# A convolution with a routed feed-forward layer: 512-row blocks with seven products, and sequences worked whole

## The chip, the cores and the metric

The kernel runs on one core of one Trainium2 chip. The metric is the device time of one execution in microseconds (us). Before the change three runs gave 1325.76, 1326.06 and 1327.54 us; the median is 1326.06 us.

## The reference

The input is `x` of 8 sequences x 3584 tokens x 192 channels, float32. First a lightweight convolution: each of 8 heads has 24 channels and seven taps, and a token's new value is the softmax-weighted sum of itself and the six tokens before it:

```
out = np.einsum('hk,bskhg->bshg', w, x_unf)      # 7 taps for each of 8 heads
```

Then each convolved token goes through one of eight feed-forward experts. Its expert is the argmax of eight logits, but where a "local" gate is at least 0.5 the token takes the expert of the token before it, so the choice runs along the sequence:

```
if s == 0 or local_gate[b, s] < 0.5: e = fresh_e
else:                                e = prev_e
h = np.maximum(x[b, s] @ w1[e], 0.0)             # 192 -> 1024
out[b, s] = p[e] * (h @ w2[e])                   # 1024 -> 192
```

There are 28672 tokens. Counted by expert, the reference's routing gives 3274, 3841, 3138, 3745, 3518, 3081, 4253 and 3822 tokens.

## The kernel before, in words

**Two jobs.** The side work convolves the tokens, finds their experts and scatters their rows into `slots`, a buffer in HBM that is sorted by expert. The main loop takes blocks of rows of one expert out of `slots` and puts them through the expert's two matrices. A unit is 128 rows. Rounded up by expert, the counts above are 229 units.

**Blocks.** The list `blocks` is fixed when the kernel is built; which expert and which rows a block takes is read at run time from small tables that the side work fills (`table`). Before the change there are 35 single blocks (128 rows), 87 pairs (256 rows) and 20 singles at the end: 55 + 174 = 229 units. Two spare singles stand behind a run-time branch.

**One block on TensorE.** `hidden` (line 952) multiplies the rows by the first matrix, 192 deep as three 64-row pieces, two array halves at a time (line 963), ReLU on ScalarE (line 968) writes `hT`. Then TensorE transposes the rows `xg` of the *next* block (`turn`, line 928; transposes recorded at line 359), which ScalarE copies to `xT` (line 949). Then `output` (line 973) multiplies `hT` by the second matrix (line 980); ScalarE and VectorE scale the two halves and add them into `o_sb` (lines 988, 992), and GpSimd scatters the rows to the output (line 996). TensorE takes its instructions in order: the transposes for block i+1 stand between the two products of block i.

**Transfers.** SyncE's queue loads weights (line 904, 1.5 MB a block, three blocks ahead), input (line 119) and rows (`load_rows`, line 911). The first load of a group of tokens waits until every scatter ("put", line 775) of the group into `slots` has landed. Scatters and output scatters go through GpSimd's one in-order queue.

**Side work.** 16 groups of 1792 tokens, two to a sequence. Groups 0 and 1 go through TensorE at the start. Groups 2 to 15 are convolved on VectorE: per head one ScalarE tap (line 377) and six VectorE instructions (line 387), 48 a group, 128 x 336 elements each. Then `route` transposes and multiplies by the gate (line 580, 24 matmul pairs, "logits"), finds experts and positions, and adds 14 puts to `to_put`. All of it is dealt out in the main loop by hand: `step(t)` emits about t us of side work into VectorE's queue at fixed places of a block. `ensure(i)` emits the row loads up to three blocks ahead; where the group of a block isn't routed and put yet, it goes away and tries again a block later, until only two blocks are left; then it emits side work and puts at once, whatever is behind them.

Of the kernel before, what the change touches and what calls it, by code (L numbers as in the profile page):

```python
# [8 lines left out]
F32 = mybir.dt.float32  # L9
# [8 lines left out]
P = 128  # L18
# [15 lines left out]
NX = NT + HALO  # L34
# [4 lines left out]
KT = BT // P  # L39
# [4 lines left out]
EARLY = 3  # L44
SPARE = 2

# [5 lines left out]


ONE = [_sure(min(g + 1, EARLY) * PT, UT) for g in range(NPART)]
TWO = [_sure((g + 1) * PT - ONE[-1] * UT, BT) if g >= EARLY else 0 for g in range(NPART)]


HALF = 0.5
FULL = {0: ONE[0], HALF: _sure(PT + PT // 2, UT), **{g: ONE[g] for g in range(1, NPART)}}
REST = NU - ONE[-1] - 2 * TWO[-1]  # L60
# [21 lines left out]
def kernel(  # L82
# [13 lines left out]
    xs = ctx.enter_context(tc.tile_pool(name="xs", bufs=2))  # L96
    ys = ctx.enter_context(tc.tile_pool(name="ys", bufs=4))
# [3 lines left out]
    xp = ctx.enter_context(tc.tile_pool(name="xp", bufs=6))  # L101
    tp = ctx.enter_context(tc.tile_pool(name="tp", bufs=1))
    hp = ctx.enter_context(tc.tile_pool(name="hp", bufs=1))
    op = ctx.enter_context(tc.tile_pool(name="op", bufs=2))
    xps_p = ctx.enter_context(tc.tile_pool(name="xps_p", bufs=1, space=PSUM))
    hps_p = ctx.enter_context(tc.tile_pool(name="hps_p", bufs=4, space=PSUM))
    yps_p = ctx.enter_context(tc.tile_pool(name="yps_p", bufs=2, space=PSUM))
# [6 lines left out]
    def load_x(g):  # L114
        x_sb = xs.tile([P, NX, D], F32, name="x_sb")
        src = x[g // PER]
        win = bass.AP(tensor=src.tensor, offset=src.offset + g % PER * PT * D,
                      ap=[[NT * D, P], [1, NX * D]])
        nc.sync.dma_start(out=x_sb.rearrange("p t d -> p (t d)"), in_=win)
        return x_sb  # L120

    def load_b(g):

        x_sb = xs.tile([P, NX, D], F32, name="x_sb")
        xv = x_sb.rearrange("p t d -> p (t d)")[:, :NB * D].rearrange("p (b d) -> p b d", d=D)
        for b in (slice(0, NH), slice(NH, NB)):
            nc.sync.dma_start(out=xv[:, b, :], in_=xb[g, :, b, :])
        return xv
# [9 lines left out]
    with tc.tile_pool(name="scr", bufs=1) as scr:  # L138
# [4 lines left out]
        x_in = {0: load_b(0)}  # L143
        wg = cst.tile([P, 3 + DQ, Q], F32, name="wg")
        nc.sync.dma_start(out=wg, in_=wgl)
        x_in[1] = load_b(1)
# [43 lines left out]
    def z_tile():  # L190
        return yt.tile([P, 3 * NH * TB + NB * DR], F32, name="z")
# [3 lines left out]
    def wide(g, xv, y_sb, both):  # L195
# [58 lines left out]
        yr = zy[:TB, 3 * NH * TB:].rearrange("p (b d) -> p b d", d=DR)  # L254
# [17 lines left out]
        lt = sm.tile([P, NB, E + 1], F32, name="lt")[:TB]  # L272
# [9 lines left out]
    pi = cst.tile([P, 2], I32, name="pi")  # L282
    nc.gpsimd.iota(pi, pattern=[[0, 2]], base=0, channel_multiplier=1)
    ti0 = cst.tile([P, NT], I32, name="ti0")
    nc.gpsimd.iota(ti0, pattern=[[1, NT]], base=0, channel_multiplier=NT)
# [10 lines left out]
    pf = cst.tile([P, 2], F32, name="pf")  # L296
    nc.gpsimd.tensor_copy(pf, pi)
    nc.gpsimd.tensor_tensor(pf[:, 1:], pf[:, 1:], pf[:, :1], op=Alu.add)
# [32 lines left out]
    cum = cst.tile([P, 1 + E * NT], F32, name="cum")  # L331
# [5 lines left out]
    nc.sync.dma_start(out=slots[DUMMY * UT:(DUMMY + 1) * UT], in_=pad)  # L337
# [8 lines left out]
    tab = [cst.tile([P, 3], F32, name=f"tab{k}") for k in range(3)]  # L346
    ends = [cst.tile([P, 1 + E], F32, name=f"ends{k}") for k in range(3)]
    for k in range(3):
        nc.gpsimd.memset(tab[k], 0.0)
        nc.gpsimd.memset(ends[k], 0.0)  # L350
# [12 lines left out]
    def row_tile():  # L363
        return ys.tile([P, NB, DG], F32, name="y_sb")

    def conv(g, x_sb):
        y_sb = row_tile()[:, :NT, :]
        got[g] = y_sb

        def cols(h):  # L370
            return y_sb[:, :, Y0 + h * GS:Y0 + (h + 1) * GS]

        def chans(h, k):
            return x_sb[:, k:k + NT, h * GS:(h + 1) * GS]

        def first(h):
            nc.scalar.activation(cols(h), chans(h, 0), Act.Copy, scale=c[:, h, 0:1])  # L377

        first(0)
        yield 0  # L380
        for h in range(H):
            if h + 1 < H:
                first(h + 1)
            if h == H // 2 and 2 < g < NPART - 1:
                x_in[g + 1] = load_x(g + 1)
            for k in range(1, KC):
                nc.vector.scalar_tensor_tensor(cols(h), chans(h, k), c[:, h, k:k + 1],  # L387
                                               cols(h), Alu.mult, Alu.add)
                yield 0.6
# [3 lines left out]
    def wide_route(g, y_sb, lt):  # L393
# [16 lines left out]
        ex = sm.tile([P, NB, E], F32, name="ex")[:TB]  # L410
# [3 lines left out]
        eq = sm.tile([P, NB, E], F32, name="eq")[:TB]  # L414
# [13 lines left out]
        def norm():  # L428
            nc.vector.tensor_reduce(rs, ex, axis=AX.X, op=Alu.add)
            nc.vector.tensor_scalar(rs, rs, 1e-9, None, Alu.add)  # L430
            nc.vector.reciprocal(rs, rs)
# [42 lines left out]
        upto = sm.tile([P, E, 1 + NB], F32, name="upto")  # L474
# [90 lines left out]
    def logits(g, y_sb):  # L565

        z = z_tile()[:, :NT * D].rearrange("p (t d) -> p t d", d=D)
        for t in range(0, NT, TQ):
            u = min(t + TQ, NT)
            nc.vector.transpose(z[:, t:u, :], y_sb[:, t:u, Y0:Y0 + D])  # L570
            yield 0.2 * (u - t)
        yield "hop"


        lps = [hps_p.tile([P, TQ * Q], F32, name="hps") for half in range(2)]
        begin = [min(TQ * j, NT - TQ) for j in range(4)]
        for b in range(DQ):
            for j in range(4):
                for half, rows in halves():
                    nc.tensor.matmul(lps[half][Q * j:Q * j + Q, :], lhsT=wgq[rows, b, :],  # L580
                                     rhs=z[rows, begin[j]:begin[j] + TQ, b * Q:(b + 1) * Q],
                                     start=(b == 0), stop=(b == DQ - 1))
        ls = sm.tile([P, 2, TQ * Q], F32, name="ls", bufs=1)
        for half in range(2):
            nc.scalar.copy(ls[:, half, :], lps[half])  # L585
        yield "hop"
        lq = sm.tile([P, 2 * TQ, Q], F32, name="lq", bufs=1)
        nc.vector.transpose(lq.rearrange("p t e -> p (t e)"), ls.rearrange("p h x -> p (h x)"))  # L588
        yield 0.4
        lt = sm.tile([P, NT + 2, E + 1], F32, name="lt")  # L590
        for r in range(4):
            for j in range(4):
                t, u = TQ * j, min(TQ * (j + 1), NT)
                at = r // 2 * TQ + t - begin[j]
                e0 = r % 2 * (E + 1)
                nc.vector.tensor_copy(lt[Q * r:Q * r + Q, t:u, :],  # L596
                                      lq[Q * j:Q * j + Q, at:at + u - t, e0:e0 + E + 1])
                yield 0.12
        return lt

    def route(g):
        y_sb = got.pop(g)
        lt = yield from logits(g, y_sb)
        lg = lt[:, :NT, :E]
        mx = sm.tile([P, NT], F32, name="mx")
        nc.vector.tensor_reduce(mx, lg, axis=AX.X, op=Alu.max)
        yield 0.3
        ex = sm.tile([P, NT, E], F32, name="ex")
        nc.vector.tensor_tensor(ex, lg, bcast(mx, E), op=Alu.subtract)
        yield 0.3  # L610

        eq = sm.tile([P, NT, E], F32, name="eq")
        nc.vector.scalar_tensor_tensor(eq, ex, 0.0, bcast_mid(ed, NT), Alu.is_equal, Alu.mult)
        yield 0.3
        key = sm.tile([P, NT], F32, name="key")
        nc.vector.tensor_reduce(key, eq, axis=AX.X, op=Alu.max)
        yield 0.3
# [616 lines left out]
```

## Time and profile before

| what | us |
|---|---|
| profiled execution, whole | 1326.81 |
| its span, first to last instruction | 1325.1 |
| TensorE busy in the span | 1304.4 |
| start, up to the first matmul of block 0 | 46.2 |
| 35 singles | 213.9 |
| 87 pairs | 948.7 |
| 20 singles | 109.5 |
| from the last matmul to the end | 6.8 |

The engines are PE (TensorE; PEld is its weight load), DVE (VectorE), ACT (ScalarE), POOL (GpSimd) and SP (SyncE). A row of the timeline gives start and length in us, engine, line, operation, tiles and count; behind it, in brackets, the idle time before and what ended it. The profile records each 64-row matmul of the program as two instructions. "Granted clock" is the share of full speed that TensorE's throttle allowed.

### The profile page before, as it was taken

To read this page: it belongs to the slowest core of one execution; us is meant where nothing else is said; L and a number is where in the kernel's file an instruction comes from. 1 tells how busy PE (TensorE), PEld (TensorE's weight loads), DVE (VectorE), ACT (ScalarE), POOL (GpSimd) and SP (SyncE) were. 2 spreads that over 40 slices of the span, in tenths; PEclk is the share of its full clock that TensorE was granted. 3 is DMA by queue.
4 is the path that set the end of the run, shared out by engine and by line. 5 is a ranking of instruction groups with operands and counts; after the bars stand their busy time and mean duration, and the time that the engine had idled before them with its cause. 6 is when DMAs were issued, how large, how long until landed. Compare 5 with 4: busy or idle time off the path is not lost. (4 is left out here: it accounts for less than half of the span.)

```text
span 1325.1 us, 41356 instructions
## 1 busy us (share of the span) xinstructions
PE 1304.4 (98%) x16682; PEld 1260.9 (95%) x16682; DVE 778.3 (59%) x2434; ACT 625.2 (47%) x1571; POOL 480.4 (36%) x520
## 2 busy tenths in 40 slices
PE   9899999999999999999999999999999999999997
PEld 7799999999999999999999999999999999999997
DVE  6888898977878787878777878785610000000000
ACT  5345555544454545444545454544444444444553
POOL 4445352534343434343434343434344212211111
PEclk9999999999999999999999999999999999999999
DMA  5789999967575757575757575756565555556893
GB/s 188 283 349 391 376 365 345 394 213 266 182 275 177 290 188 277 201 260 192 271 186 273 193 271 199 267 195 210 197 211 205 189 185 188 192 187 229 313 317 131
DMA packets 67298, 325.29 MB, mean 245 GB/s; under 512 B 12576, under 2 KB 38103, under 8 KB 47650
## 3 DMA queue, kind: packets, MB, share of 16 engines
q1 hardware_dynamic: 44784, 277.41, 58.4%
q0 software_dynamic: 22320, 45.22, 9.2%
q8 instruction: 133, 2.18, 0.7%
q14 instruction: 59, 0.48, 0.1%
q10 hardware_dynamic: 2, 0.00, 0.0%
HBM read 277.29 MB, written 45.77 MB: 244 GB/s over the span
## 5 line engine op out<-in xcount | busy, mean ns | idle before, releaser
L980 PE MATMUL yps<-wb,hT 64*128 64x192 f32 x7328 | 641.0, 325 | 5.8 <-ACT hT L968 2.8
L963 PE MATMUL hps<-xT,wb 64*128 64x256 f32 (+1 forms) x6816 | 637.2, 336 | 1.7 <-issue 1.4
L963 PEld LDWEIGHTS hps<-xT,wb 64*128 64x128 f32 x6816 | 589.1, 187 | 27.2 <-issue 4.0
L980 PEld LDWEIGHTS yps<-wb,hT 64*128 64x128 f32 x7328 | 602.8, 187 | 11.1 <-issue 4.6
L996 POOL DMA_INDIRECT out_dram<-o_sb,xg x229 | 232.3, 1014 | 605.7 <-DVE o_sb L992 533.9
L968 ACT ACTIVATE hT<-hps 128x512 f32<-128x512 f32 (+1 forms) x568 | 261.9, 512 | 361.4 <-PE hps L963 246.5
L387 DVE SCALAR_TENSOR_TENSOR y_sb<-x_sb,c,y_sb 128x336 f32<-128x336 f32 x672 | 376.5, 570 | 18.9 <-issue 0.8
L992 DVE SCALAR_TENSOR_TENSOR o_sb<-yps,xg,o_sb 128x192 f32<-128x192 f32 x229 | 87.5, 414 | 467.8 <-ACT o_sb L988 461.4
L775 POOL DMA_INDIRECT slots<-y_sb,posi x228 | 231.2, 1014 | 209.3 <-ACT xT L949 114.8
L988 ACT ACTIVATE o_sb<-yps,xg 128x192 f32<-128x192 f32 x229 | 86.9, 418 | 289.8 <-PE yps L980 287.4
L949 ACT COPY xT<-xps 64x256 f32<-64x256 f32 (+4 forms) x568 | 210.8, 371 | 11.7 <-issue 1.7
L377 ACT ACTIVATE y_sb<-x_sb,c 128x336 f32<-128x336 f32 x112 | 63.7, 581 | 0.0
L359 PEld LDWEIGHTS xps<-ident,xg 64*128 64x128 f32 (+1 forms) x916 | 57.0, 124 | 5.2
L359 PE MATMUL xps<-ident,xg 64*128 64x64 f32 (+1 forms) x916 | 60.0, 217 | 0.0
L570 DVE STREAM_TRANSPOSE z<-y_sb 128x768 f32<-128x768 f32 (+1 forms) x56 | 45.4, 853 | 0.4
L596 DVE COPY lt<-lq 32x36 f32<-32x36 f32 x224 | 40.8, 182 | 3.5
L580 PE MATMUL hps<-z,wg 64*32 64x128 f32 x1344 | 24.2, 272 | 1.2 <-issue 1.2
L580 PEld LDWEIGHTS hps<-z,wg 64*32 64x32 f32 x1344 | 19.2, 105 | 4.1 <-issue 2.9
L556 PE MATMUL yps<-y_sb,hot 112*128 112x194 f32 x64 | 12.6, 353 | 1.4 <-DVE hot L550 1.1
L556 PEld LDWEIGHTS yps<-y_sb,hot 112*128 112x128 f32 x64 | 11.3, 202 | 2.1 <-DVE hot L550 1.6
L672 DVE COPY bk<-so_far 1x32 f32<-1x32 f32 x56 | 12.3, 220 | 0.7
L588 DVE STREAM_TRANSPOSE lq<-ls 128x256 f32<-128x256 f32 x14 | 6.2, 441 | 10.9 <-ACT ls L585 10.9
(236 smaller groups left out, 358.0 us busy)
## 6 DMA issues: line engine op xcount, KB each, us to landing
wb<-in_w_dram SPq DMA_DIRECT2D x138, 1536.0 KB
x_sb<-in_x_dram SPq DMA_DIRECT2D x14, 1920.0 KB
xg<-slots SPq DMA_DIRECT2D x87, 195.0 KB
wb<-in_w_dram SPq DMA_DIRECT2D x12, 512.0 KB
xg<-slots SPq DMA_DIRECT2D x53, 97.5 KB
out_dram<-o_sb,xg POOLq DMA_INDIRECT x229
slots<-y_sb,posi POOLq DMA_INDIRECT x228
x_sb<-in_xb_dram SPq DMA_DIRECT2D x4, 768.0 KB
```

What stands on the lines that cost most here:

```text
L359: nc.tensor.transpose(to, src[rows], identity=ident[rows, rows])
L377: nc.scalar.activation(cols(h), chans(h, 0), Act.Copy, scale=c[:, h, 0:1])
L387: nc.vector.scalar_tensor_tensor(cols(h), chans(h, k), c[:, h, k:k + 1], cols(h), Alu.mult, Alu.add)
L570: nc.vector.transpose(z[:, t:u, :], y_sb[:, t:u, Y0:Y0 + D])
L775: ins = nc.gpsimd.indirect_dma_start(out=slots[:, :], in_=rows, in_offset=None, out_offset=bass.IndirectOffsetOnAxis(ap=to, axis=0)).ins
L949: copied = nc.scalar.copy(a, b)
L963: nc.tensor.matmul(hps[half][:, j, w], lhsT=wb[rows, f0:f0 + P], rhs=xT[rows, d, w], start=(d == 0 and j == 0), stop=(d == KD - 1), skip_g ...
L968: relu = nc.scalar.activation(hT[:, m:m + 2, w], hps[half][:, :, w], Act.Relu)
L980: nc.tensor.matmul(yps[half][:, k * D:(k + 1) * D], lhsT=hT[rows, m, k * P:(k + 1) * P], rhs=wb[rows, WA + m * D:WA + (m + 1) * D], start= ...
L988: nc.scalar.activation(o_sb[:, k, :], y[k][0], Act.Copy, scale=xg[:, k, 0:1])
L992: nc.vector.scalar_tensor_tensor(o_sb[:, k, :], y[k][1], xg[:, k, 0:1], o_sb[:, k, :], Alu.mult, Alu.add)
L996: sent = nc.gpsimd.indirect_dma_start(out=out, in_=o_sb[:, k, :], in_offset=None, out_offset=bass.IndirectOffsetOnAxis(ap=xg.bitcast(I32)[ ...
```

## The change

1. **Blocks of 512 rows.** Of the later rows 18 blocks of four units are made (`seven`). The first product of such a block splits rows and hidden columns in two and does seven products in place of eight for two of the three pieces of depth; counted in calls of 256 columns it makes 11 in place of the 12 that two pairs make. For that, sums of weights are made on GpSimd (`combine_w`, 4 instructions of 128 x 256), sums of rows on VectorE (`combine_x`, 5 of 128 x 256), and sums of results by ScalarE copies and VectorE additions of 128 x 1024 (3 each).
2. **Another list of blocks.** 35 singles, 49 pairs, 18 of 512 rows, 5 pairs, 14 singles: 35 + 98 + 72 + 10 + 14 = 229 units. How many blocks are full is now guessed (`_likely`), and 26 spare singles stand behind the branch for a guess that fails.
3. **Side work.** Groups 2 to 5 stay as they were, but their input comes one head at a time. From the fourth sequence on a whole sequence (28 tokens a partition) is convolved and routed at once: 48 VectorE instructions of 128 x 672 for 3584 tokens, and 28 puts. The logits of a sequence are two parts of 14, and each part's matmuls are cut in two halves around the first half of a block's `output` (`visit`).
4. **`ensure`** now goes away only while more than one block is left (two for singles), and then emits the missing puts at once.
5. **PSUM.** Four pools of two banks (`wps_p`, `zps_p`, `yps_p`, `xps_p`) take the place of the three that were there; the row buffers `xg` are five and 512 rows wide.

```diff
-EARLY = 3
+EARLY = 6
+XG = 5
...
+PAIRED = 49
...
+TWO = {g: min(PAIRED, _likely((g + 1) * PT - ONE[LAST] * UT, BT, LEFT2)) if g >= SINGLE else 0
+       for g in GROUPS}
...
+    def combine_w(wb):
...
+        wt = hp.tile([P, 3, 2 * P], F32, name="wt")
+        b11, b12, b21, b22 = [wb[:, k * 2 * P:(k + 1) * 2 * P] for k in range(4)]
+        nc.gpsimd.tensor_tensor(wt[:, 1, :], b22, b12, op=Alu.subtract)
+        yield
+        nc.gpsimd.tensor_tensor(b12, b12, b11, op=Alu.subtract)
...
+    def seven(wb, wt, xT, xc, turn_next, weights_next):
...
+        times(xb, a11, b11, True)
+        nc.scalar.copy(h11, xb)
+        times(yb, s1, t1, True)
+        times(yb, a23, b32)
+        nc.scalar.copy(h22, yb)
+        times(xb, s2, t2)
+        nc.scalar.copy(h12, xb)
+        put(times(wbk, a12, b21, True))
+        times(wbk, a13, b31)
+        step(SIDE[0], None, 1)
+        nc.vector.tensor_tensor(h11, wbk, h11, op=Alu.add)
+        nc.scalar.activation(h11, h11, Act.Relu)
+        put(times(xb, s3, t3))
+        nc.vector.tensor_tensor(h22, xb, h22, op=Alu.add)
+        nc.scalar.activation(h22, h22, Act.Relu)
+        times(yb, s4, b22)
+        put(times(yb, s5, b32))
+        at = turn_next()
+        times(xb, a22, t4)
...
         for j in range(len(xgs) + i, min(i + AHEAD + 1, len(blocks))):
             g = blocks[j][3]
             while st["routed"] < g or any(p[0] <= g for p in to_put):
-                if j > i + 2:
+                if j > i + (2 if blocks[i][1] == 1 else 1):
                     return
-                step(4.2)
+                if st["routed"] < g:
+                    step(4.2, wps_p)
                 put()
             xgs[j] = load_rows(j)
```

## The prediction

> **What bounds the kernel now.** I read the page first, then busy time by stage, then the timeline of single blocks, last the waits. The page's first part:
>
> ```profile
> PE 1304.4 (98%) x16682; PEld 1260.9 (95%) x16682; DVE 778.3 (59%) x2434; ACT 625.2 (47%) x1571; POOL 480.4 (36%) x520
> ```
>
> TensorE works through. By stage (singles, pairs, last singles; columns: length, busy us of each engine, clock, DMA share, GB/s):
>
> ```profile
> 46.20:260.10 213.90, 206.56 (x3331) 200.45 (x3330) 187.74 (x566) 114.40 (x355) 96.38 (x96) 1.00 0.94 358
> 260.10:1208.80 948.70, 947.67 (x11400) 915.50 (x11398) 549.79 (x1737) 433.11 (x979) 342.33 (x337) 1.00 0.62 219
> 1208.80:1318.30 109.50, 109.24 (x1680) 108.68 (x1676) 8.68 (x21) 54.95 (x177) 20.47 (x21) 1.00 0.79 276
> ```
>
> It holds in every stage; VectorE has 187.7 of 213.9 us in the singles, where DMA has 0.94, and half of the time in the pairs. The chain of waits is no help here (it stops at the last scatter). One pair of the timeline:
>
> ```profile
> 1006.38 5.34 PE L963 MATMUL hps<-xT,wb 64*128 64x256 f32 x48
> ...
> 1011.56 0.39 PE L359 MATMUL xps<-ident,xg 64*128 64x64 f32 x8
> ...
> 1011.79 5.42 PE L980 MATMUL yps<-wb,hT 64*128 64x192 f32 x64
> ...
> 1016.88 5.10 PEld L963 LDWEIGHTS hps<-xT,wb 64*128 64x128 f32 x48
> 1017.04 5.34 PE L963 MATMUL hps<-xT,wb 64*128 64x256 f32 x48
> ```
>
> Starts, not lengths, give the cost: first product 5.18 us (48 records, 0.108 each), transposes 0.23, second product 5.25; a pair is 10.66 us without a gap. A single, read the same way at 1302.00 and 1307.44, is 5.44. So 35 singles should take 190.6 and took 213.9 (23.3 over); 87 pairs 927.9, and took 948.7 (20.8 over). The logits, 14 times 1.73 us (24.2 busy at line 580), are in that; some 20 us are gaps.
>
> **The change, part by part.**
>
> *Seven products.* A 512-row block has 11 calls of 8 records, 88 x 0.108 = 9.50, 16 transposes 0.46, and two second products 10.50: 20.46 us. Two pairs are 21.33. So 18 x 0.87 = **-15.6**, if nothing in the block makes TensorE wait. The new operations have no row of their own. ScalarE's 128 x 1024 copy: from line 968 (128x256 381 ns, 128x512 595) the slope gives 1.02 us. VectorE's 128 x 1024 addition: with the slope of line 550 (128 columns of line 682 275 ns, 112x512 691) 1.22 us; with the dearer PSUM rows (line 992, 192 columns, 414) 1.9. Laid along TensorE's calls (0.86 each), the copy of the third call is ready at 4.9 us and needed at 5.2, the second addition at 7.9 and needed at 8.3, at 1.9 us each only at 9.2. So 0 to 1 us a block; I take 0, since these are plain long instructions and line 550 is the nearest row, and keep 18 in the range. The row sums (5 on VectorE) come behind the first scatter of the block, 2 us ahead of their use. GpSimd's four sums: the one-input copy of line 223 (112x512, 655 ns) bounds one by 0.3 and 1.3 us; 1.3 to 5.2 a block beside four scatters at 1.29 = 5.2, in 20.5 us: hidden. If GpSimd were late, the second call would wait.
>
> The Trainium skill, GPSIMD Engine Reference, "Elementwise — side-by-side cycle accounting", has a two-input operation there at about half of VectorE's pace, 4497 ns for 2048 elements. By that one sum is an estimated 0.6 to 0.7 us, and the total stays as it is.
>
> *Other blocks.* Six singles become three pairs: 3 x 10.66 - 6 x 5.44 = **-0.7**. Units stay 229: counted from the reference's routing, every one of the 49 + 18 + 5 guessed blocks is full, so no spare runs.
>
> *Logits.* 14 parts as before. One moves from the singles (3.1 us over a bare block there, e.g. 8.42 for 5.44) to the pairs (2.1): **-1.0**.
>
> *Side work on VectorE.* The row to scale:
>
> ```profile
> L387 DVE SCALAR_TENSOR_TENSOR y_sb<-x_sb,c,y_sb 128x336 f32<-128x336 f32 x672 | 376.5, 570 | 18.9 <-issue 0.8
> ```
>
> At 672 columns it is 0.92 us by the slope above, 1.14 in proportion; I take 0.95. The built order puts side work into blocks 0 to 80 and three idle pairs behind. Summed over the 40 busiest pairs it is 400 us of VectorE at 0.95 and 446 at 1.14, against 442 of TensorE (426.6 and nine logits). So VectorE goes from 58% to 90% there, and the cost is 0, at worst 5. Nothing in a block needs it sooner than 5 us.
>
> *Two row loads that come late.* This is what I expect to decide. In the built order all but two groups are put well before their rows are loaded. At block 54 (a pair), three puts of the fourth sequence are still open and are emitted at once; at block 83, the last pair before the 512-row blocks, eight of the last sequence. They stand in GpSimd's queue behind the two output scatters of the block before, and those wait for that block's result. The load waits for the puts to land, and the transposes wait for the load, in the middle of the block, with the second product behind them. The steps, in the timeline:
>
> ```profile
> 421.04 1.05 POOL L775 DMA_INDIRECT slots<-y_sb,posi  x1 [1.85 <-ACT xT L949]
> 423.97 1.68 SPq L911 DMA_DIRECT2D xg<-slots  x2
> 424.69 2.69 PE L963 MATMUL hps<-xT,wb 64*128 64x256 f32 x22
> 425.34 0.74 DVE L992 SCALAR_TENSOR_TENSOR o_sb<-yps,xg,o_sb 128x192 f32<-128x192 f32 x2 [0.83 <-ACT o_sb L988]
> 426.03 0.99 POOL L996 DMA_INDIRECT out_dram<-o_sb,xg  x1 [3.94 <-DVE o_sb L992]
> ```
>
> The first output scatter starts 1.34 us into the next block (424.69 to 426.03). A row load goes out 1.9 us after the last put ends (422.09 to 423.97; elsewhere 1.5 and 2.5). Two scatters stand 1.29 apart (415.37, 416.66), and free puts 1.25:
>
> ```profile
> 28.66 0.94 POOL L775 DMA_INDIRECT slots<-y_sb,posi  x1 [0.30 <-issue]
> 29.91 0.94 POOL L775 DMA_INDIRECT slots<-y_sb,posi  x1 [0.30 <-issue]
> ```
>
> From the trace's packets, a 195 KB load issued at 347.94 ended at 350.38 (first packet at 348.89, 1.05 us a load once it flows): 2.4 us, and for 390 KB 0.95 + 2.1 + 0.3 = 3.4. Block 54: 1.34 + 2 x 1.29 + 3 x 1.25 - 0.3 = 7.4, + 1.9 + 2.4 = 11.7; the first product is over at 5.2: **+6.5** (bounds 4.9 to 9.5). Block 83: 1.34 + 2.58 + 10.0 - 0.3 = 13.6, + 1.9 + 3.4 = 18.9, - 5.2 = **+13.7** (10.3 to 15.6). In the old kernel such loads had one more block, 10.66 us, which is why the timeline above shows no stop.
>
> *The clock after a stop.* In the start TensorE idled 1.9 us, and then ran at half clock:
>
> ```profile
> 39.10:41.00 1.90, 0.00 (x0) 0.00 (x0) 1.73 (x9) 1.01 (x4) 1.32 (x2) 1.00 1.04 417
> ...
> 43.00:46.40 3.40, 3.40 (x14) 3.15 (x14) 3.26 (x8) 0.88 (x4) 1.58 (x2) 0.50 1.03 413
> ```
>
> Both new stops are longer: 3.4 us at half clock lose 1.7 each, **+3.4** (0 to 3.4).
>
> The Trainium skill, TensorE: Matmul & The Clock Gate, "Part 1: The HAM clock gate", says that it takes an idle window of about 3.4 us to halve the clock. The row above shows it after less, with the window not tied to the stop. By the page the first stop might go free, which would be 1.7 us less.
>
> *Start and end.* The order of the start moves (all of `gather(1)` ahead of the first transposes, transposes of block 2 behind block 1); the gaps there were 3.0 us at block 0 and 2.4 at block 2. I leave it at 0, with 4 either way.
>
> **Sum.** -15.6 - 0.7 - 1.0 + 6.5 + 13.7 + 3.4 = +6.3. The profiled execution took 1326.81 (1.7 of it outside the span) and would take 1333.1; it lay 0.75 above the median, so against the median of the runs I say 1332.
>
> **Rivals.** *The gaps go too (faster).* Of the 20 us of gaps, those of late ScalarE and VectorE work may vanish: taps are now issued behind the scaling of the output, and logits in two halves. For: ReLU stood behind a tap that waited at 116.33. Against: most gaps are 0.3 to 0.6 us of "issue", which stay. If 10 to 20 go, it is 1312 to 1322, say 1317; it decides from 9 us on.
>
> *The 512-row blocks are paced by ScalarE and VectorE (slower).* At 1.9 us an addition the third call into the first bank waits 1 us in each of 18 blocks: the gain is gone and the two stops stay, 1342 to 1350. It decides from 1.55 us an addition; the slope of line 550 speaks against it.
>
> *It doesn't do what it says:* a guessed block that isn't full costs a block and a spare, over 10 us. The counts exclude it.
>
> *The loads aren't late.* Should the puts land before the first product ends, 23.6 us go, and it is 1309. I see no room for it: they can't start before the output scatters do.
>
> **Chances.** Two late loads eat the gain, 1332 (1326 to 1339): 0.50. Gaps gone: 0.26. Loads not late: 0.07. Blocks paced: 0.17. Range: 1311 to 1344. A run can tell 0.2% (2.65 us) from no change. Faster, below 1323.4: 0.33; within: 0.12, from the lower end of the first case; slower: 0.55.
>
> **What would show it.** Right: TensorE idle 6 and 13 us, in front of line 398, in the 20th and the 49th pair; a 512-row block every 20.5 us; no side work behind block 80; VectorE near 90% in the pairs. Wrong: 512-row blocks of 21 us and more with TensorE waiting for VectorE or ScalarE in line 1128; no idle before those transposes; pairs of over 10.7 us throughout; or a start that moved by more than 4 us.

## The result, and the profile after

The changed kernel takes **1371.58 us** (median of 4 runs, 1369.33 to 1372.06); the kernel before took 1326.80 beside it. The ratio is 1.033 (1.031 to 1.035): 45 us slower, where 6 were forecast, and outside the range. The profiled execution took 1371.87 us, its span 1370.2.

The page's first part, and the busy time by stage (35 singles; 49 pairs; 18 blocks of 512 rows; columns as before: length, busy us of PE, PEld, DVE, ACT and POOL, granted clock, DMA share, GB/s):

```profile
PE 1314.1 (96%) x16394; PEld 1244.3 (91%) x16394; DVE 758.5 (55%) x1912; ACT 651.5 (48%) x1412; POOL 570.1 (42%) x598
```

```profile
45.87:271.64 225.77, 213.03 (x3233) 203.03 (x3234) 175.68 (x554) 113.11 (x356) 88.87 (x89) 0.98 0.93 332
271.64:863.38 591.74, 563.62 (x6948) 523.00 (x6946) 419.83 (x1019) 256.66 (x559) 305.76 (x268) 0.98 0.64 224
863.38:1230.71 367.33, 367.33 (x4171) 355.58 (x4170) 124.17 (x211) 200.95 (x270) 130.25 (x145) 1.00 0.33 117
```

TensorE has fewer instructions than before (16394 for 16682), yet its busy time rose by 9.7 us, and its clock fell below 1.00 in the first two stages: busy time that grows because instructions last longer is not more work. The third stage is clean: 18 blocks of 20.4 us.

The starts of the blocks give a ledger. Each block is counted from its first matmul to the next block's. A "bare" block, one without logits and without a wait, takes 5.44 us as a single, 10.66 as a pair and 20.42 with 512 rows; what a block takes over that is put where it arose:

| us | before | after | difference | forecast |
|---|---|---|---|---|
| bare blocks | 1226.6 | 1209.8 | -16.8 | -16.3 |
| blocks 54 and 83, over bare | 0 | 26.2 | +26.2 | +23.6 |
| 14 logits blocks, over bare | 31.6 | 49.2 | +17.6 | -1.0 |
| blocks 0 to 6 (without logits), over bare | 6.5 | 15.4 | +8.9 | 0 |
| all other blocks, over bare | 7.4 | 14.5 | +7.1 | 0 |
| start, and end behind the last matmul | 52.9 | 55.0 | +2.1 | 0 |

The sum is +45.1, the difference of the spans. Two lines hold what was forecast; the next three, +33.6 us, do not.

**The two stops**, in the timeline of PE, POOL and SyncE's queue. Block 54:

```profile
487.39 5.45 PE L1076 MATMUL ps<-xT,wb 64*128 64x256 f32 x48
...
488.10 0.99 POOL L1194 DMA_INDIRECT out_dram<-o_sb,xg  x1 [3.96 <-DVE o_sb L1189]
...
493.22 0.96 POOL L871 DMA_INDIRECT slots<-y_sb,posi  x1 [0.30 <-issue]
...
497.03 2.08 SPq L1016 DMA_DIRECT2D xg<-slots  x3
...
499.50 0.69 PE L398 MATMUL ps<-ident,xg 64*128 64x64 f32 x8 [6.66 <-DMA xg<-slots]
```

Block 83:

```profile
838.36 0.99 POOL L1194 DMA_INDIRECT out_dram<-o_sb,xg  x1 [0.30 <-issue]
...
849.80 0.96 POOL L871 DMA_INDIRECT slots<-y_sb,posi  x1 [0.30 <-issue]
...
853.51 3.41 SPq L1016 DMA_DIRECT2D xg<-slots  x3
...
856.13 1.12 PE L398 MATMUL ps<-ident,xg 64*128 64x64 f32 x16 [14.99 <-DMA xg<-slots]
```

Read each upward from its last line: the transposes waited 6.66 and 14.99 us for the row load, the load went out 2.8 us after the last put of its group ended, and the puts stood behind two output scatters (the row at 488.10 is the first of one pair, that at 838.36 the first of the other).

**The pauses.** Block 67, a pair without logits:

```profile
652.12 0.96 POOL L871 DMA_INDIRECT slots<-y_sb,posi  x1 [0.30 <-issue]
...
653.38 0.96 POOL L871 DMA_INDIRECT slots<-y_sb,posi  x1 [0.30 <-issue]
...
654.65 0.96 POOL L871 DMA_INDIRECT slots<-y_sb,posi  x1 [0.30 <-issue]
...
655.22 1.04 PE L1173 MATMUL ps<-wb,h 64*128 64x192 f32 x4 [0.81 <-issue]
...
656.65 1.59 PE L1173 MATMUL ps<-wb,h 64*128 64x192 f32 x16 [0.39 <-issue]
```

PE waits here for nothing that the profile shows ("issue"), and between such waits it gets only a few matmuls. The block takes 13.35 us for 10.66. GpSimd is in the middle of a row of scatters 1.26 us apart.

**One thing has to be known of the runs below.** They are timed beside the kernel before, in batches of up to four kernels on one chip (the expectations speak of a call, an allocation or a chip). The batches fell into two kinds: in some the kernel before took 1315 to 1316 us and no such pauses are in the traces; in others it took 1327 to 1333 us and they are there, as in this profile. The chips numbered 3 and 12 each had both kinds; what sets the kind was not found. Ratios hold within a batch only.

### The profile page after: what moved, and what is told of

Same layout as the page of the kernel before. It is cut to its first block, busy times and chain, and to the rows that moved or that the text cites. A ratio compares the mean times of both kernels' runs of the same rounds, so it can differ in the third digit from the quotient of the medians.

```text
span 1370.2 us, 40368 instructions
## 1 busy us (share of the span) xinstructions
PE 1314.1 (96%) x16394; PEld 1244.3 (91%) x16394; DVE 758.5 (55%) x1912; ACT 651.5 (48%) x1412; POOL 570.1 (42%) x598
## 3 DMA queue, kind: packets, MB, share of 16 engines
q8 instruction: 132, 2.16, 0.7%
## 5 line engine op out<-in xcount | busy, mean ns | idle before, releaser
L1173 PE MATMUL ps<-wb,h 64*128 64x192 f32 x7328 | 643.2, 328 | 7.4 <-issue 4.0
L1173 PEld LDWEIGHTS ps<-wb,h 64*128 64x128 f32 x7328 | 606.6, 189 | 17.0 <-issue 12.9
L1076 PE MATMUL ps<-xT,wb 64*128 64x256 f32 (+1 forms) x4944 | 438.0, 328 | 3.9 <-issue 2.3
L1076 PEld LDWEIGHTS ps<-xT,wb 64*128 64x128 f32 x4944 | 397.6, 187 | 30.4 <-issue 7.1
L464 DVE SCALAR_TENSOR_TENSOR y_sb<-x_sb,c,y_sb 128x672 f32<-128x672 f32 (+1 forms) x432 | 325.6, 762 | 67.5 <-ACT y_sb L423 45.9
L1189 DVE SCALAR_TENSOR_TENSOR o_sb<-ps,xg,o_sb 128x192 f32<-128x192 f32 x229 | 86.9, 412 | 404.1 <-ACT o_sb L1183 396.4
L1080 ACT ACTIVATE h<-ps 128x512 f32<-128x512 f32 (+1 forms) x412 | 181.2, 493 | 262.6 <-PE ps L1076 155.9
L1183 ACT ACTIVATE o_sb<-ps,xg 128x192 f32<-128x192 f32 x229 | 86.4, 418 | 339.6 <-PE ps L1173 315.7
L1054 ACT COPY xT<-ps 128x256 f32<-128x256 f32 (+2 forms) x484 | 197.4, 408 | 22.0 <-PE ps L398 14.4
L1128 PE MATMUL ps<-xT,wb 64*128 64x256 f32 x864 | 102.7, 376 | 0.0
L1128 PEld LDWEIGHTS ps<-xT,wb 64*128 64x128 f32 x864 | 86.7, 187 | 5.3
L665 PEld LDWEIGHTS ps<-z,wg 64*32 64x32 f32 x1344 | 21.4, 107 | 16.9 <-issue 15.6
```

The lines of the kernel that those rows point to most:

```text
L464: nc.vector.scalar_tensor_tensor(cols, x_in[u][:, k:k + n, :], c[:, h, k:k + 1], cols, Alu.mult, Alu.add)
L1054: copied = nc.scalar.copy(a, b)
L1076: nc.tensor.matmul(hps[:, half, j, :], lhsT=wb[rows, f0:f0 + P], rhs=xT[rows, d, :], start=(d == 0 and j == 0), stop=(d == KD - 1), skip_g ...
L1080: relu = nc.scalar.activation(hT[two][:, half], hps[:, half], Act.Relu)
L1128: ins = nc.tensor.matmul(to[:, half, j, :], lhsT=b[rows, j * P:(j + 1) * P], rhs=a[rows, :], start=(first and j == 0), stop=True, skip_gro ...
L1173: ins = nc.tensor.matmul(yps[:, half, k * D:(k + 1) * D], lhsT=h[two][rows, side, j, k * P:(k + 1) * P], rhs=wb[rows, WA + f * D:WA + (f + ...
```

## The experiments

The headings or the text say of which kind a batch was.

### One to four: parts undone (without pauses, before 1315.24)

**Logits in one piece.**

```diff
-                if b == DQ // 2:
-                    yield "half"
...
-            st["bank"], st["due"], st["half"] = bank, False, True
+            st["bank"], st["due"], st["half"] = bank, False, False
```

> The 24 matmul pairs of a logits part stand in one piece, still in the middle of the first half of a block's output. Theory A (the cut into two halves is what made a logits block dearer: twice as many changes between short and long matmuls, each with pauses of issue, and a halved clock after two of them): the 14 logits blocks, 49.2 us over bare blocks, go back towards the 31.6 us of the kernel before; 1371.6 - 15 = 1356 us, 1352 to 1362. Theory B (the pauses come with the short matmuls themselves or with the place in the middle of the output, not with the cut): the same sum in one place, 1368 to 1375 us.

Measured: 1330.31 us, ratio 1.011 (1.009 to 1.013).

**Two more pairs ahead of the 512-row blocks**: `PAIRED = 51` in place of 49.

> 51 pairs ahead of 17 blocks of 512 rows, so that the first row load that needs the last sequence comes two pairs later and finds its puts emitted. Theory A (the stop at block 83 is the forced puts behind the output scatters): its 16.9 us go, and one block of 512 rows less costs 0.9: 1371.6 - 16.0 = 1355.6 us, 1353 to 1359. Theory B (the stop is the first load of 390 KB itself, behind weights in its queue): it moves to block 85 and stays, 1370 to 1374 us.

Measured: 1323.85 us, ratio 1.006 (1.004 to 1.008).

**Puts sooner.**

```diff
-            if n == 2 and two and len(to_put) > (16 if k else 4):
+            if n == 2 and two and len(to_put) > (4 if k else 0):
```

> A pair takes puts at its two last places from 5 and from 1 open put on, not from 17 and 5, so that none is left over at block 54. Theory A (three forced puts make the stop at block 54): its 9.3 us go, 1362.3 us, 1360 to 1365; the stop at block 83 stays, since eight puts are still forced there. Theory B (GpSimd's queue is full, and sooner puts make the output scatters of these pairs late instead): 1368 to 1376 us, the time of the stop spread over the pairs 49 to 53 and 56 to 61.

Measured: 1329.84 us, ratio 1.011 (1.010 to 1.013).

**No seven products**: `FOUR = 0` and `LOST = 0`.

> Pairs in place of the 18 blocks of 512 rows, nothing else changed. Theory A (the seven products gain 0.90 us a block, and the loss lies elsewhere): 18 x 0.90 = 16.2 us more, less 1.0 for a smaller late load at block 83: 1386.8 us, 1384 to 1390. Theory B (the 512-row blocks cost as much elsewhere as they save, in the weights' sums on GpSimd or in what follows them): 1368 to 1376 us.

Measured: 1348.26 us, ratio 1.025 (1.023 to 1.026).

The expectations were made from 1371.6 us, a time with pauses, and this batch had none; so what counts is the length of single blocks. They say:

- With 51 pairs block 83 is a plain pair, but block 85 takes 6.8 us too much, though no put is forced there: puts that are emitted in time can be done late. The last put ended at 819.63, as block 85 began (819.51), the load went out 2.6 us later, and it took another 6.0 us, for 2.6 at block 83 before; so theory B, the slow first load, has a part in what is left. Sooner puts cut block 54 from 10 us over bare to 3.8 and leave 17.6 at block 83. The late loads are shown; each was expected to vanish whole, and a part remained (6.8 and 3.8 us).
- Without the seven products the list holds 36 pairs of 10.66 (383.8) for 18 blocks of 20.42 (367.6): the gain of 16.2 us is real.
- Logits in one piece take 1.7 to 2.2 us over a pair, cut in two 2.0 to 2.4. The pauses are gone here with both versions, so the cut by itself does not make them; **my first theory of the excess fell here.** In batches with pauses the logits in one piece were no better (runs seven and eleven below).

The same logits of block 60 with pauses (first profile), and without (the run with sooner puts):

```profile
568.85 0.44 PE L665 MATMUL ps<-z,wg 64*32 64x128 f32 x13
...
570.21 0.45 PE L665 MATMUL ps<-z,wg 64*32 64x128 f32 x7 [0.43 <-issue]
...
570.98 0.49 PE L665 MATMUL ps<-z,wg 64*32 64x128 f32 x11 [0.32 <-issue]
...
571.75 0.53 PE L665 MATMUL ps<-z,wg 64*32 64x128 f32 x16 [0.28 <-issue]
...
572.21 4.55 PE L1173 MATMUL ps<-wb,h 64*128 64x192 f32 x32
```

```profile
541.92 1.13 PE L665 MATMUL ps<-z,wg 64*32 64x128 f32 x48
...
542.99 2.87 PE L1173 MATMUL ps<-wb,h 64*128 64x192 f32 x32
```

Half of a part, 48 records, takes 3.4 us in place of 1.1, and then the 32 records of the output take 4.55 in place of 2.87, for the most part at half clock.

### Five to eight: the same kernels again, and all three edits (with pauses, before 1327.79)

> The changed kernel once more, beside the others of this call. In the four runs before it the kernel before took 1315.2 us in place of 1326.8, and the pauses of issue in the split logits, 4 us a block at worst in the first profile, were not there. Theory C (those pauses belong to the chip of the first runs, not to the change; the late loads belong to the change): from the run with sooner puts, 1329.8 + 6.5 for block 54 = 1336 us, 1332 to 1341, ratio 1.016. Theory D (they belong to the change, and each edit took some away): ratio 1.033, 1358 us where the kernel before takes 1315.

Measured: 1373.19 us, ratio 1.032 (1.028 to 1.036).

> The kernel before once more, for its trace beside that of the changed kernel on the same chip. Theory C: on the chip where it takes 1315 us, the pauses of issue are gone here too, start, singles and pairs together 11 us shorter than in the first profile (singles 213.9, pairs 948.7), and logits blocks stay at 1.9 us over a pair. Theory D: the same stages shrink evenly, by 0.9% each, as by a faster clock.

Measured: 1328.96 us, ratio 1.001. The changed kernel's loss of 45 us is repeated in this batch, on chip number 12. That the pauses belong to one chip (theory C) was shown wrong later, when number 12 had none.

Logits in one piece, and puts at four places of a pair, with 50 and with 51 pairs:

```diff
-            if n == 2 and two and len(to_put) > (16 if k else 4):
+            if n == 2 and len(to_put) > (8 if not two else 4 if k else 0):
```

> All three edits: logits in one piece, puts at four places of a pair while more than eight are open, and 50 pairs ahead of 18 blocks of 512 rows (4 behind them, in place of 5), so that no puts are forced. Theory A (two late loads and the cut make the loss): from 1336 us on a chip where the kernel before takes 1315, 17.6 less for block 83, 10 for block 54, 4.5 for the logits: 1304 us, 1300 to 1309, ratio 0.991. Theory B (GpSimd's queue is the limit: seven puts a block and two output scatters fill 11 of 10.7 us, and rows or outputs come late in these pairs): 1312 to 1325.

> The same with 51 pairs and 17 blocks of 512 rows, one more pair between the last puts and the load that needs them. Theory A: 0.9 more than with 50 pairs, 1305 us. Theory B (puts that are emitted in time but done late still hold the load, as 6.8 us at block 85 with 51 pairs showed): 1 to 5 us less than with 50 pairs.

Measured: **1395.29** us, ratio 1.051 (1.048 to 1.053), and 1393.95, ratio 1.049 (1.046 to 1.052). Both miss widely: 0.991 was expected for the first. With 50 pairs the two stops are gone (block 54 under 0.3 us over bare, block 83 4.3), but the pairs in which puts stand closest, up to seven one behind another, have grown: blocks 50, 60, 67 and 75 are 9.2, 11.3, 12.9 and 15.7 us over bare, for 1.7, 6.4, 3.6 and 7.8 in the changed kernel itself in the same batch. In this trace the pauses in the pairs lie in or right behind a row of scatters. That gave theory E: **scatters in a row hold TensorE's instructions back.**

### Nine to eleven: scatters added and spread (with pauses, before 1329.02)

```diff
+    PLAN = {1: ("burst", 3), 2: ("burst", 5), 3: ("burst", 7), 4: ("every", 2), 5: ("every", 3)}
...
+            if how == "burst" and call[0] == 4:
+                for _ in range(much):
+                    extra(ins)
+            if how == "every" and call[0] % much == 0:
+                extra(ins)
```

> The changed kernel with extra scatters of 128 zero rows into a buffer of their own, in ten of the 18 blocks of 512 rows, whose 20.42 us are otherwise exact: 3, 5 and 7 in a row behind the fifth call (two blocks each), six of them 1.7 us apart, four 2.6 us apart; the other eight blocks have none. Theory E (while GpSimd issues scatters 1.25 us apart, TensorE gets its instructions late, from the third on): blocks with 3 stay at 20.4 to 20.6, with 5 take 1 to 2 us more, with 7 take 3 to 5 more; the spaced ones stay at 20.4. Theory F (the pauses of blocks 50, 60, 67 and 75 come with the side work of VectorE or the input loads, and only coincide with the scatters): all at 20.4. On a chip like that of the first four runs, blocks 0 to 83 will have no pauses of issue and the extra scatters should cost nothing under either.

Busy time by block, one 512-row block to a line: 3, 5, 7 and 7 extra scatters in a row, six 1.7 us apart, four 2.6 us apart:

```profile
921.59:942.00 20.41, 20.41 (x235) 19.92 (x234) 7.00 (x12) 11.13 (x15) 10.12 (x11) 1.00 0.37 133
...
963.40:984.94 21.54, 21.04 (x237) 20.70 (x236) 7.01 (x12) 11.24 (x15) 12.18 (x14) 1.00 0.38 137
984.94:1010.33 25.39, 23.55 (x236) 22.40 (x235) 7.01 (x12) 11.24 (x15) 13.94 (x15) 0.93 0.35 123
1010.33:1036.78 26.45, 24.78 (x235) 23.13 (x233) 7.00 (x12) 11.24 (x15) 13.79 (x15) 0.87 0.32 115
1036.78:1059.25 22.47, 21.79 (x237) 20.66 (x236) 7.10 (x12) 11.13 (x15) 13.18 (x15) 1.00 0.38 136
...
1081.39:1102.40 21.01, 20.64 (x235) 20.46 (x234) 7.01 (x12) 11.24 (x15) 11.08 (x12) 1.00 0.37 133
```

Theory E is shown by doing it: nothing but the extra scatters differs between these blocks, and they cost 0, 1.1, 5.0 and 6.0 us. Three in a row are free, as expected, and seven cost a little more than expected. The two with seven also lose the clock (0.93 and 0.87, one and two windows of 3.41 us at half clock, 1.7 us each); without that loss seven cost 3.3 and 2.6 us. The spaced ones, expected free, cost 2.0 and 0.6; but of the six the first four still went out 1.27 us apart, right behind the two output scatters. The profiled and only run took 1391.77 us.

A long row is not enough; its scatters must also stand close. The profile of the changed kernel shows it in blocks 57 to 59, three pairs (the first line is busy time, columns as before; the others are from block 58):

```profile
528.69:560.69 32.00, 32.00 (x363) 29.84 (x362) 25.03 (x32) 15.74 (x33) 26.21 (x20) 1.00 0.81 279
...
541.15 1.59 POOL L871 DMA_INDIRECT slots<-y_sb,posi  x1 [0.30 <-issue]
543.04 1.48 POOL L871 DMA_INDIRECT slots<-y_sb,posi  x1 [0.30 <-issue]
544.83 1.63 POOL L1194 DMA_INDIRECT out_dram<-o_sb,xg  x1 [0.31 <-DVE y_sb L464]
```

Here 19 scatters follow one another without a break, but most last 1.4 to 1.6 us in place of 0.96, so that they start up to 1.94 us apart and never more than three at 1.3 or less. The three pairs take 32.00 us, which is bare. The pauses of block 67 come in a row of five that start 1.26 to 1.30 us apart, two outputs and three puts. VectorE is busy for 25.0 of these 32 us, so its side work alone (theory F) does not make the pauses.

Puts spread, and 56 pairs ahead of 15 blocks of 512 rows:

```diff
-PAIRED = 49
+PAIRED = 56
...
+    def tight():
+        return bool(to_put) and to_put[0][0] <= EARLY + 1
...
-            if shares and (n == 2 or two or len(to_put) > (NT if st["block"] % 2 else 2 * NT)
-                           or to_put and to_put[0][0] >= EARLY):
+            if shares and (n == 2 and tight() or two or n == 1 and (len(to_put) > (NT if st["block"] % 2 else 2 * NT)
+                           or to_put and to_put[0][0] >= EARLY)):
...
-            if n == 2 and two and len(to_put) > (16 if k else 4):
+            if n == 2 and two and len(to_put) > ((4 if k else 0) if tight() else (20 if k else 0)):
```

> Puts spread out: for sequences with slack three a pair (four while more than 20 are open), 1.7 us and more apart; sooner ones for block 54 as before; 56 pairs ahead of 15 blocks of 512 rows, so that the last sequence needs no forced puts. On a chip where the changed kernel takes 1373 us and the kernel before 1327.8: Theory E: the stop at block 83 goes (-17.5), three 512-row blocks less (+2.6), 5.3 at block 54, and some 20 us of pauses in blocks 60 to 82: 1333 us, ratio 1.004 (1.000 to 1.010). Theory F: pauses stay, only the stops go: 1353, ratio 1.019. On a chip without pauses: 1336 - 17.6 - 6.5 + 2.6 = 1315 us where the kernel before takes 1315.2.

> The same with each part's logits in one piece. Theory E: fewer changes of pace on TensorE, 0.3 us less in each of 14 blocks: 4 us less than with the cut, ratio lower by 0.003. Theory F (short matmuls in one piece empty the store of instructions deeper): 0 to 15 us more.

Measured: **1342.79** us, ratio 1.012 (1.009 to 1.014), and with logits in one piece 1346.66, ratio 1.015 (1.012 to 1.017). Blocks 67 and 80 to 82 are plain pairs again, block 75 is 2.7 over bare, the stop at 83 is 1.5. The changed kernel itself was not run in this batch; an estimate for it is 1391.77 less the 18.1 us that the extra scatters cost in their blocks and less the 4.9 us by which that run is longer behind its last matmul (13.96 for 9.1), 1368.8. So the edit took some 26 us off, 14 short of what was expected, and its ratio of 1.012 lies just above theory E's range. Putting the logits back into one piece gains nothing: it costs 4 us, which is what theory F of that run allowed.

### Twelve to eighteen: what kind of transfer, and is it the change

Seven extra transfers in a row, of four kinds; and the kernel before with its puts held back into 23 rows of seven:

```diff
+        if behind is not None and to_put and st["block"] >= ONE[-1]:
+            held[0] += 1
+            if held[0] % 7:
+                return
+            for _ in range(6):
+                one(behind)
+        one(behind)
```

> The changed kernel with seven extra transfers in a row behind the fifth call of eight 512-row blocks, by kind: blocks 86 and 87 scatters of 780-byte rows by GpSimd, as in the run before; 88 and 89 scatters of 4-byte elements by GpSimd; 90 and 91 plain writes of 128 x 780 bytes on SyncE's queue; 92 and 93 the same plain writes on GpSimd's queue. Theory G (what delays TensorE's instructions is the making of a scatter, 128 addresses at a time): 86 to 89 take 4 to 6 us more, 90 to 93 nothing. Theory H (it is the traffic of many small packets): 86, 87 and 90 to 93 take 4 to 6 us more, 88 and 89 less than 1. Theory I (it is GpSimd's queue, whatever it sends): 86 to 89, 92 and 93 take 4 to 6 us more, 90 and 91 nothing. On a chip without the pauses, none takes more.

> The kernel before with its puts held back in the pairs until seven go out in a row, 20 runs of seven in place of twos and threes. Theory E (runs of scatters delay TensorE, whatever the kernel): 2 to 5 us a run, 40 to 100 us more, ratio 1.03 to 1.08. Theory F (the pauses need the changed kernel's side work): 0 to 6 us, for outputs and loads that come a little later. On a chip without the pauses: 0 to 6 us.

> The changed kernel with two spare singles behind the branch, as in the kernel before, in place of 28. From the last matmul to the end the changed kernel took 9.1 us, the kernel before 6.8. If the branch over the longer code costs it: 2.3 us less, 1369.3 us where the changed kernel takes 1371.6. If not: the same.

This batch had no pauses (before 1315.88). The kinds cost nothing: 20.4 to 20.6 us in all eight blocks; the run took 1336.86. The kernel before in rows took 1320.68, ratio 1.003 (1.002 to 1.005). Even these 4.8 us are not the rows: block 37 alone is 5.5 over bare, since TensorE waits 3.5 us there for VectorE's scaling of the output, which came behind eight instructions of side work; the other pairs with rows are bare. With few spares (`LOSE = 0`; 26 were there, not 28) the changed kernel took 1331.83, ratio 1.012 (1.010 to 1.014), and from the last matmul to the end 6.7 us, as in the kernel before: the branch over the spares' code is the 2.4 us.

> The seven extra transfers by kind once more, for an allocation in which the pauses of issue are there (the kernel before then takes 1327 to 1329 us, not 1315 to 1316; the last call had none, and no kind cost anything). With the pauses: theory G (making a scatter delays TensorE's instructions): blocks 86 to 89 take 4 to 6 us more, 90 to 93 nothing. Theory H (the many small packets do): 86, 87 and 90 to 93 take 4 to 6 more, 88 and 89 less than 1. Theory I (GpSimd's queue, whatever it sends): 86 to 89, 92 and 93 take 4 to 6 more, 90 and 91 nothing. Without the pauses: 20.4 to 20.6 everywhere, as in the last call.

This batch had them (before 1328.36). Blocks 85 to 90, and 92: no extra, twice scattered rows, twice scattered single elements, plain writes by SyncE, plain writes by GpSimd:

```profile
881.99:902.41 20.42, 20.42 (x236) 19.98 (x234) 7.01 (x12) 11.24 (x15) 7.21 (x8) 1.00 0.33 118
902.41:925.99 23.58, 21.57 (x235) 20.17 (x234) 7.01 (x12) 11.24 (x15) 13.94 (x15) 1.00 0.37 131
925.99:952.50 26.51, 24.46 (x236) 23.50 (x234) 7.01 (x12) 11.24 (x15) 13.83 (x15) 0.87 0.32 116
952.50:974.98 22.48, 21.70 (x235) 20.67 (x234) 7.01 (x12) 11.24 (x15) 13.91 (x16) 1.00 0.31 106
974.98:1000.37 25.39, 23.40 (x236) 22.35 (x235) 7.01 (x12) 11.24 (x15) 14.03 (x16) 0.93 0.31 96
1000.37:1020.79 20.42, 20.42 (x236) 20.39 (x234) 7.01 (x12) 11.24 (x15) 7.20 (x9) 1.00 0.49 151
...
1041.21:1061.63 20.42, 20.42 (x235) 20.39 (x234) 7.01 (x12) 11.23 (x15) 11.05 (x15) 1.00 0.45 152
```

Theory G fits best: rows cost 3.2 and 6.1 us, elements of 4 bytes 2.1 and 5.0 (the first block of each below its forecast), plain writes of the same bytes nothing, on either queue, though they load the DMA engines more (0.49 and 0.45 for 0.37). So it is not the traffic, and what is left is GpSimd's making of a scatter. But the plain writes on GpSimd's queue were not a row of the same length: six went out within 3.3 us, 0.55 us each, and the seventh 1.5 or 3.8 us later, where seven scatters take 8.6 us, and three scatters were free too. That a longer row of plain writes by GpSimd would cost as much (theory I) is not excluded. The Trainium skill, Perfetto Trace Analysis, "DMA Instruction — SWDGE (GPSIMD)", says that GpSimd's own processors make the descriptors of such a transfer, and that its span in the profile ends when the last is made. By that the 0.96 us of each scatter are its making; how it reaches TensorE's instructions no run here shows.

> The kernel before with its puts in runs of seven, once more. With the pauses, theory E (runs of scatters delay TensorE in any kernel): 40 to 100 us more, ratio 1.03 to 1.08; theory F (only beside the changed kernel's side work): 4 to 8 us more, as in the last call (1320.7 against 1315.9). Without the pauses: 5 us more again.

Measured, in the same batch: **1470.56** us, ratio 1.107 (1.105 to 1.109). The kernel before, with the same work in another order, loses 142 us, 5.2 of it in block 37 again and some 6 for each of 23 rows; its clock is 0.961. So the pauses do not need the change: rows of scatters in the old kernel make them too.

> Logits in one piece, puts at four places of a pair, 50 pairs, no forced puts, once more. With the pauses it takes 1395 us again (ratio 1.05). Without them: the changed kernel takes 1334 there (1331.8 with few spares, and 2.3); less 17.3 for block 83, 10 for block 54 and 4 for the logits: 1303 us, 1299 to 1309, ratio 0.990, faster than both kernels.

> The same kernel a third time, for a call without the pauses (the kernel before at 1315 to 1316 us): 1303 us, 1299 to 1309, ratio 0.990, faster than both kernels. With the pauses (the kernel before at 1327 to 1329): 1392 to 1395 us as twice before, ratio 1.05, and whether the three edits win without them stays open.

Measured: 1392.08, ratio 1.048 (1.046 to 1.050), and 1402.82, ratio 1.053 (1.051 to 1.055); both batches had the pauses (the latter on chip number 3, which had none at first). Whether these edits beat the kernel before without pauses stays open, and no version here beat it.

## Why the prediction was wrong, step by step

**Seven products, -15.6: right.** 20.42 us a block for 20.46; 18 x (21.32 - 20.42) = -16.2. The instructions taken by slope lasted as forecast (ScalarE's copies 1.01 to 1.02 us for 1.02; VectorE's below):

```profile
L464 DVE SCALAR_TENSOR_TENSOR y_sb<-x_sb,c,y_sb 128x672 f32<-128x672 f32 x240 | 218.0, 916 | 40.6 <-ACT y_sb L423 23.7 <-issue 7.2 <-DMA slots<-y_sb,posi 3.6
...
L1143 DVE TENSOR_TENSOR h<-ps,h 128x1024 f32<-128x1024 f32 x18 | 22.0, 1224 | 67.4 <-PE ps L1128 67.4
```

0.92 us for 0.95, and 1.22 for 1.22. (Line 682's row, from which the slope was taken, has 112 columns and not 128; the 1.22 comes out with 112.) The sums on GpSimd took 0.73 us, within the bounds and a little above the 0.6 to 0.7 estimated from the page. With the other blocks, the bare blocks are 16.8 us less for 16.3.

**VectorE at 90%, cost 0: the cost right, the share not.** The work was as summed, 407.4 us for 400, but it lay in the 529.1 us of blocks 36 to 80, 77% of them; ordinary pairs stayed at 10.66.

**Late load at block 54, +6.5: right** (6.66 idle), the mechanism by the timeline, the closeness partly by luck. Its parts moved against each other: the first output scatter came at 0.7 us, not 1.34, the load went out 2.8 after the last put, not 1.9.

**Late load at block 83, +13.7: right** (14.99, in its bounds). The surplus is two puts ahead of the output scatters, which began 2.6 us into the block; the load went out 0.9 later and landed 0.8 faster than forecast.

**The clock after a stop, 2 x 1.7: low.** The two blocks are 26.2 us over bare, 21.7 of it idle: 4.6 for 3.4. The first stop did not go free: from 497.46 to 504.28 the clock was halved, behind a window in which TensorE had been idle throughout. But four more windows at half clock came with the pauses and a third late load, 1.7 us each, and the forecast had none of them. The two windows around the logits of block 60:

```profile
569.14:572.55 3.41, 2.16 (x51) 1.14 (x41) 3.28 (x4) 0.00 (x0) 2.80 (x2) 1.00 0.87 261
572.55:575.96 3.41, 3.41 (x26) 3.41 (x24) 1.31 (x2) 0.00 (x0) 1.10 (x2) 0.50 0.14 45
```

There was no stop, only pauses: 2.16 us busy in 3.41, and the next 3.41 ran at half clock. It does not always follow: the window from 654.50, in the pauses of block 67, has 2.16 us busy too, and the clock stayed at 1.00. The Trainium skill, TensorE: Matmul & The Clock Gate, "Part 1: The HAM clock gate", calls the window free-running, and the trace agrees: 53.72, 234.63, 497.46 and 572.55, where the clock fell, are whole multiples of 3.413 us apart. That it takes an idle window is not what these two rows show.

**The logits, -1.0, and "most gaps are 0.3 to 0.6 us of issue, which stay": this is the step that failed.** The logits cost 17.6 us more, not 1.0 less, and the gaps did not stay: without the two stops, TensorE lost 55.0 us beside bare blocks and bare logits (79.2 less 24.2; 5.0 of it are the load of block 6, below), for 21.4 before. I had read "issue" as a cost of TensorE's own, and counted the 28 puts a sequence only as GpSimd's time and as what a load waits for. In the old kernel they go out in twos and threes, and its trace has little to show; in the new one a pair takes up to six (block 83 more), and with the two output scatters they make rows of five and more at 1.26 us. Four logits blocks, 18, 28, 60 and 75, are 23.9 us over bare, 15.4 more than in the run with few spares, which had no pauses; scatters stand close in each, though only three in the singles 18 and 28. The logits' short matmuls suffer most (15.6 us of issue waits of their weight loads alone). For the pairs the cause is shown by adding scatters and by spreading them; no run spread those of blocks 0, 1, 18 and 28, and there it is read from the timeline.

In batches without pauses the logits cost 2.0 to 2.2 us a pair. There the changed kernel, 1331.83 with few spares and the 2.4 us of the end, would take an estimated 1334, 18 above the kernel before: -16.8 of bare blocks, +27 of stops, 3 of logits, 2.4 of the end and some 2 in the start (the kernel before by its trace in rows of seven, without block 37). So even there 12 us more than forecast.

**Start, 0: a loss of 9 us in blocks 0 to 6.** 5.0 of them are a third late load, in block 6: the rows of block 7 were asked for at 89.23 and came at 95.1. Weights and input had been asked for at 84.44 and 84.88, and in this stage the DMA engines were 0.93 busy. It cost 4.4 to 6.9 us in all runs of the changed kernel and its variants. The kernel before asks as late (at 87.42), but its last weights had been asked for at 75.45, and it had the rows by 90.95. That the input, one head at a time, made the difference is likely and not shown: loading it in another order wasn't tried. The other 4 are pauses in blocks 0 and 1, with the half clock at 53.72.

**End, 0: +2.4**, the code of the spares.

**Rivals.** That the gaps go fell: they grew, which I had not priced. Blocks paced by VectorE and loads that aren't late fell by the lines above. Of the signs of being wrong, "a start that moved by more than 4 us" came true in blocks 0 to 6; "pairs of over 10.7 us throughout" did not: they are over it only in the blocks with close scatters.

## What to carry to other kernels

A move that packs the same transfers into less time is not free because their engine is idle: count how many indirect scatters go out at their shortest distance, here 1.26 us, and keep them to twos and threes, or further apart (up to 1.9 us was free here). "Issue" gaps on the engine that bounds the kernel can have a cause elsewhere; see what every other engine does at that moment before assuming that they stay. And a wait moved to its last moment, here a row load behind forced puts, could be priced within 1.3 us from the queue it stands in.

## What the runs showed of the hardware

- Seven indirect scatters by GpSimd 1.26 us apart, behind two output scatters, cost TensorE 2.1 to 6.1 us in a 20.42 us block (2.1 to 3.3 without the half clock that followed in some), three nothing; the size of the rows (4 or 780 bytes) matters little, and seven plain writes cost nothing. A row of 19 that start up to 1.94 us apart cost nothing.
- This comes and goes between batches, and with it about 1% of the kernel before's time (1315 to 1316, or 1327 to 1333 us); it does not go with the number of the chip. Where it is absent, the kernel before in rows of seven loses 4.8 us, by a wait in one block; where it is present, 142.
- The half clock of TensorE does not need a stop: 1.25 us of pauses in a window of 3.41 were enough in block 60, and not in block 67.
